# Weight transfers issued behind the first units' scaling, unit 0 first on every engine, and a second layer two units behind the first

## The chip, the cores and the metric

The kernel runs on one core of one Trainium2 chip. The metric is the device time in microseconds of that core; before the change three runs took 210.71, 210.63 and 213.97 us (median 210.71). The engines named below are PE (matmuls), ACT (activations), DVE (vector work), POOL (elementwise work, and the issue of the weight transfers) and SP (the issue of all other transfers). Each engine takes its instructions strictly in the order in which they are written.

## The reference, cut to what matters

A gated linear attention (a decayed state per head) feeds a two-layer perceptron with a leaky ReLU:

```python
# q, k, v, f_logit: (4, 8, 768, 48)
f = 1.0 / (1.0 + np.exp(-f_logit))
for t in range(S):
    state = f[:, :, t, :, None] * state + einsum('bhd,bhe->bhde', k[:, :, t], v[:, :, t])
    y[:, :, t] = einsum('bhd,bhde->bhe', q[:, :, t], state)
x = y.transpose(0, 2, 1, 3).reshape(B * S, H * D)       # 3072 x 384
h = x @ w_in                                            # 384 x 2048
g = np.maximum(0.01 * h, h)
return g @ w_out                                        # 2048 x 384
```

All inputs arrive as f32. The four attention inputs are 18.9 MB together, each weight matrix is 3.1 MB, and the output is 4.7 MB.

## The kernel before, in words

**Units.** The sequence of 768 steps is cut into 6 chunks of 128; a unit is one chunk of one of the 4 batch rows with all 8 heads, so there are 24 units, chunk by chunk. Units 0 to 3 are the first chunk of the four rows and have no state to read. A unit's four inputs f, k, q, v are four transfers of 192 KB each (`load`, L82), issued by SP, in runs of 48 f32 per head and step. Its output is one transfer of 192 KB (`put`, L261).

**Attention of a unit.** `gate_act` turns f into log decays lf with two activations; `gate_pe` sums them along the chunk with one matmul (into cs) and four narrow ones; `decay_act` makes the factors em and a (and a_end, but for the last chunk); `scale_pool` multiplies k by em (kh), q by a (qh) and casts v, all three on POOL. `turn_pe` transposes kh and qh on PE, `turn_dve` copies them out as kT and qbd; `score_pe` makes the scores pw, `mask_dve` masks them into wm, `mix_pe` makes the output py (for later chunks with the state too), `y_act` casts it to xn, `x_pe` transposes it, and `x_dve` copies it into xT, the input of the first layer. `state_pe`, `state_dve` and `state_pool` bring the state up to the end of the chunk.

**The two layers.** `up(u, g)` is one quarter of the first layer: 24 matmuls of 128x128 into one of two PSUM buffers pm, and one Prelu activation on ACT into gT. `down(u, half)` is half of the second layer: 8 matmuls of 128x384 into pm2, of which there is one buffer; `put` copies pm2 out on DVE and has SP store it. Of gT there are 5 buffers.

**Weights.** `load_w_in(part, 2)` issues three transfers of 256 KB on POOL (half of the columns, as bf16), `load_w_out(part, 2)` one of 768 KB. Groups 0 and 1 of `up` need the first half of w_in, groups 2 and 3 the second; the first half of `down` needs the first half of w_out.

**Order.** The order is written by hand (manual schedule): each engine's program is the order of the calls. Ahead of the loop stand the loads, then the attention of unit 0 mixed with the gates of units 1 and 2. The loop over units (L300 to L331) puts the attention of unit i+1 between the pieces of the two layers of unit i, the scaling of unit i+2 and the gate activations of unit i+3 beside them. `LA` is 5: `load(i + 5)` stands at the head of iteration i.

Of the kernel before, what the change touches and what calls it, by code (L numbers as in the profile page):

```python
# [15 lines left out]
def kernel(  # L16
# [10 lines left out]
    nc = tc.nc  # L27

    B, H, S, D = q.shape
# [9 lines left out]
    NU = len(units)  # L39
# [29 lines left out]
    qhs = [const.tile([128, H, 64], BF16, name=f"qh{i}", tag=f"qh{i}") for i in range(3)]  # L69
# [10 lines left out]
    raw = {}  # L80

    def load(u):  # L82
        c, b = units[u]
        r = {}
        for name, src in (("f", f_logit), ("k", k), ("q", q), ("v", v)):
            t = inp.tile([128, H, D], FP32, name=f"{name}_raw", tag=f"{name}_raw")
            nc.sync.dma_start(out=t, in_=src[b, :, c * C:(c + 1) * C, :].rearrange("h t d -> t h d"))
            r[name] = t
        raw[u] = r

    def load_w_in(part, parts):
        w = FF // parts
        for kk in range(NK):
            nc.gpsimd.dma_start(out=w_in_b[:, kk, part * w:(part + 1) * w],  # L94
                                in_=moe_w_in[kk * 128:(kk + 1) * 128, part * w:(part + 1) * w])

    def load_w_out(part, parts):
        n = NF // parts
        nc.gpsimd.dma_start(  # L99
            out=w_out_b[:, part * n:(part + 1) * n, :],  # L100
            in_=moe_w_out[part * n * 128:(part + 1) * n * 128, :].rearrange("(a p) n -> p a n", p=128))

    st = {}


    def gate_act(u):
        f = raw[u]["f"]
        e = work.tile([128, H, D], FP32, name="e_t", tag="e_t")
        nc.scalar.activation(e, f, AF.Exp, scale=-1.0)  # L109
        lf = lfs[u % 3]  # L110
        nc.scalar.activation(lf[:, :, 0:D], e, AF.Ln, bias=1.0)  # L111

    def gate_pe(u):
        c, b = units[u]
        lf = lfs[u % 3]
        cs = ps_s.tile([128, 512], FP32, name="cs", tag="sm")
        nc.tensor.matmul(cs[:, 0:H * D], ut, lf[:, :, 0:D], start=True, stop=True)  # L117
        if c < NCH - 1:
            for p in range(P2):
                nc.tensor.matmul(cs[:, H * D + p:H * D + p + 1], lf[:, 2 * p:2 * p + 2, :], ones_col,  # L120
                                 start=True, stop=True)
        st[u] = {"cs": cs}

    def decay_act(u):
        c, b = units[u]
        cs = st[u]["cs"]
        a_t = work.tile([128, H, D], BF16, name="a_t", tag="a_t")
        em_t = work.tile([128, H, D], BF16, name="em_t", tag="em_t")
        nc.scalar.activation(em_t, cs[:, 0:H * D], AF.Exp, scale=1.0)  # L129
        nc.scalar.activation(a_t, cs[:, 0:H * D], AF.Exp, scale=-1.0)  # L130
        if c < NCH - 1:
            a_end = work.tile([128, P2], FP32, name="a_end", tag="a_end")
            nc.scalar.activation(a_end, cs[:, H * D:H * D + P2], AF.Exp, scale=-1.0)
            st[u]["a_end"] = a_end
        st[u]["a"], st[u]["em"] = a_t, em_t

    def scale_pool(u):
        r = raw.pop(u)
        nc.gpsimd.tensor_mul(khs[u % 3][:, :, 0:D], r["k"], st[u]["em"])  # L139
        nc.gpsimd.tensor_mul(qhs[u % 3][:, :, 0:D], r["q"], st[u]["a"])  # L140
        v_b = work.tile([128, H, D], BF16, name="v_b", tag="v_b")
        nc.gpsimd.tensor_copy(out=v_b, in_=r["v"])  # L142
        st[u]["v"] = v_b

    def turn_pe(u):
        tp = ps_t.tile([128, 2, P2, 128], BF16, name="tp", tag="tp")
        for i, src in enumerate((khs[u % 3], qhs[u % 3])):
            for p in range(P2):
                nc.tensor.transpose(tp[:, i, p, :], src[:, 2 * p:2 * p + 2, :], ident)  # L149
        st[u]["tp"] = tp  # L150
# [27 lines left out]
    def mix_pe(u):  # L178
        c, b = units[u]
        s = st[u]  # L180
        qbd, v_b, wms = qbds[u % 2], s["v"], s.pop("wm")
        py = ps_s.tile([128, 512], FP32, name="py", tag="sm")
        n = H if c == 0 else 2 * H
        i = 0
        if c > 0:
            for h in range(H):
                nc.tensor.matmul(py[:, h * D:(h + 1) * D], qbd[:, h // 2, h % 2, :], state_b[b][:, h // 2, :],  # L187
                                 start=(i == 0), stop=(i == n - 1))
                i += 1
        for h in range(H):  # L190
            nc.tensor.matmul(py[:, h * D:(h + 1) * D], wms[h // 4][:, h % 4, :], v_b[:, h, :],  # L191
                             start=(i == 0), stop=(i == n - 1))
            i += 1
        s["py"] = py

    def state_pe(u):
        c, b = units[u]
        if c == NCH - 1:
            return
        kh, v_b = khs[u % 3], st[u]["v"]  # L200
        pt = ps_s.tile([128, P2, 2 * D], FP32, name="pt", tag="sm")
        for p in range(P2):
            nc.tensor.matmul(pt[:, p, :], kh[:, 2 * p:2 * p + 2, :], v_b[:, 2 * p:2 * p + 2, :],  # L203
                             start=True, stop=True)
        st[u]["pt"] = pt
# [18 lines left out]
    def y_act(u):  # L224
        xn = work.tile([128, KD], BF16, name="xn", tag="xn")
        nc.scalar.copy(out=xn, in_=st[u].pop("py")[:, 0:KD])  # L226
        st[u]["xn"] = xn

    def x_pe(u):
        xn = st[u].pop("xn")  # L230
        px = ps_s.tile([128, NK, 128], BF16, name="px", tag="sm")
        for kk in range(NK):
            nc.tensor.transpose(px[:, kk, :], xn[:, kk * 128:(kk + 1) * 128], ident)  # L233
        st[u]["px"] = px

    def x_dve(u):
        xT = work.tile([128, NK, 128], BF16, name="xT", tag="xT", bufs=6)
        nc.vector.tensor_copy(out=xT, in_=st[u].pop("px"))  # L238
        st[u]["xT"] = xT


    def up(u, g):
        s = st[u]
        if g == 0:
            s["g"] = gpool.tile([128, NF, 128], BF16, name="gT", tag="gT")
        pm = ps_m.tile([128, 4, 128], FP32, name="pm", tag="pm")
        for i in range(4):
            ff = 4 * g + i
            for kk in range(NK):
                nc.tensor.matmul(pm[:, i, :], w_in_b[:, kk, ff * 128:(ff + 1) * 128], s["xT"][:, kk, :],  # L250
                                 start=(kk == 0), stop=(kk == NK - 1))
        nc.scalar.activation(s["g"][:, 4 * g:4 * g + 4, :], pm, AF.Prelu, alpha=0.01)  # L252

    def down(u, half):
        s = st[u]
        if half == 0:
            s["pm2"] = ps_o.tile([128, KD], FP32, name="pm2", tag="pm2")
        for ff in range(8 * half, 8 * half + 8):
            nc.tensor.matmul(s["pm2"], s["g"][:, ff, :], w_out_b[:, ff, :], start=(ff == 0), stop=(ff == NF - 1))  # L259

    def put(u):  # L261
        c, b = units[u]
        osb = opool.tile([128, KD], FP32, name="osb", tag="osb")
        nc.vector.tensor_copy(out=osb, in_=st[u]["pm2"])  # L264
        nc.sync.dma_start(out=out[b * S + c * C:b * S + (c + 1) * C, :], in_=osb)
        st.pop(u)


    LA = 5
    load(0)  # L270
    load_w_in(0, 2)
    load(1)
    load_w_in(1, 2)
    load_w_out(0, 2)
    load_w_out(1, 2)
    for u in range(2, LA):
        load(u)

    gate_act(0)
    gate_act(1)  # L280
    gate_pe(0)
    decay_act(0)
    scale_pool(0)
    gate_pe(1)
    decay_act(1)
    scale_pool(1)
    gate_act(2)
    turn_pe(0)
    turn_dve(0)
    score_pe(0)  # L290
    mask_dve(0)
    mix_pe(0)
    state_pe(0)
    y_act(0)
    state_dve(0)
    state_pool(0)
    x_pe(0)
    x_dve(0)

    for i in range(NU):  # L300
        n1, n2, n3 = i + 1, i + 2, i + 3
        if i + LA < NU:
            load(i + LA)
        if n1 < NU:
            turn_pe(n1)
            turn_dve(n1)
        up(i, 0)
        up(i, 1)
        if n1 < NU:
            score_pe(n1)  # L310
            mask_dve(n1)
        if n2 < NU:
            gate_pe(n2)
            decay_act(n2)
            scale_pool(n2)
        up(i, 2)
        up(i, 3)
        if n1 < NU:
            mix_pe(n1)
            y_act(n1)  # L320
            state_pe(n1)
            state_dve(n1)
            state_pool(n1)
        if n3 < NU:
            gate_act(n3)
        down(i, 0)
        if n1 < NU:
            x_pe(n1)
            x_dve(n1)
        down(i, 1)  # L330
        put(i)  # L331


# [28 lines left out]
```

## Time and profile before

| | |
|---|---|
| three runs, us | 210.71, 210.63, 213.97 |
| the profiled execution, first to last instruction | span 209.4 us (its own device time is not listed; the two lowest runs are 1.2 and 1.3 us above this span) |
| busy: PE, ACT, DVE, POOL | 177.8, 108.7, 97.4, 76.8 us |
| first `up` matmul, last `down` matmul ends | 33.73 us, 206.08 us |
| DMA | 27.12 MB, of them 3.15 MB weights as written |
| granted clock of PE | 1.000 |

The profiler records one execution. Starts are microseconds from the first instruction of the span. In the view in order of time, a bracket at a row's end gives the idle time of that engine just before it, and what ended it. The chain of waits is followed back from the last instruction. The rows are shown in the prediction, where they are used.

### The profile page before, as it was taken

Reading aid. Unit: us, or ns where it says so; the run is one execution under the profiler, and the core shown is the slowest. Engines: PE = TensorE matmul, PEld = TensorE weight load, DVE = VectorE, ACT = ScalarE, POOL = GpSimd, SP = SyncE. Lnnn points to the kernel's source line nnn. Section 1 sums busy time; section 2 is a strip of 40 time slices with the busy share of each in tenths; the row PEclk is TensorE's granted clock in tenths of the full one; section 3 lists DMA queues with packets and bytes.
Section 4 is the critical chain, followed back from the end, with each engine's and each line's share of the span. In section 5 each row is a group of like instructions: output and inputs, shape, how many; then the busy total and the mean of one; then the engine's idle time right before and its main releaser. Section 6 shows DMA issues by size and latency. Waiting matters only on the chain.

```text
span 209.4 us, 5831 instructions
## 1 busy us (share of the span) xinstructions
PE 177.8 (85%) x2432; PEld 146.1 (70%) x2432; DVE 97.4 (46%) x223; ACT 108.7 (52%) x237; POOL 76.8 (37%) x129
## 2 busy tenths in 40 slices
PE   0000149999999999999999999999999999999993
PEld 0000028788779788877988887798888778877881
DVE  8000044466546545654654565465455545633511
ACT  4000332775576458447645845774585567555540
POOL 8300071542553255145325524532552454034000
PEclk9999999999999999999999999999999999999999
DMA  6999999998796479568647846956695681100111
GB/s 114 171 195 184 199 191 189 156 219 163 121 176 143 105 136 177 114 118 163 147 102 133 186 111 116 157 116 141 128 187 113 119 153 41 38 28 18 38 41 38
DMA packets 106267, 27.12 MB, mean 130 GB/s; under 512 B 100352, under 2 KB 105472, under 8 KB 106240
## 3 DMA queue, kind: packets, MB, share of 16 engines
q1 hardware_dynamic: 103296, 23.60, 59.5%
q0 software_dynamic: 2944, 3.15, 9.0%
q8 instruction: 19, 0.31, 0.6%
q14 instruction: 8, 0.07, 0.1%
HBM read 25.17 MB, written 4.72 MB: 143 GB/s over the span
## 4 chain that ended last, share of the span: by engine, by line
PE 83%; issue 10%; POOL 4%; DVE 1%; ACT 0%; POOLq 0%
PE pm L250 32%; PE pm L259 30%; PE pw L168 6%; PE tp L149 5%; PE py L191 2%; PE px L233 2%; PE py L187 2%; PE cs L117 2%; PE pt L203 2%; POOL w_in_b L94 2%; POOL w_out_b L99 1%; POOL kh L139 1%; PE cs L120 1%; DVE wm L175 1%; POOL qh L140 1%
## 5 line engine op out<-in xcount | busy, mean ns | idle before, releaser
L252 ACT ACTIVATE gT<-pm 128x512 bf16<-128x512 f32 x96 | 56.2, 601 | 64.1 <-PE pm L250 62.3
L250 PE MATMUL pm<-xT,w_in_b 128*128 128x128 bf16 x1152 | 73.4, 221 | 0.0
L259 PE MATMUL pm<-w_out_b,gT 128*128 128x384 bf16 x384 | 70.1, 326 | 0.0
L250 PEld LDWEIGHTS <-w_in_b 128*128 128x128 bf16 x1152 | 67.2, 99 | 0.6
L139 POOL TENSOR_TENSOR kh<-k_raw,em_t 128x384 bf16<-128x384 f32 x24 | 22.0, 916 | 110.5 <-ACT em_t L129 105.7
L259 PEld LDWEIGHTS <-gT 128*128 128x128 bf16 x384 | 35.2, 98 | 18.8
L175 DVE TENSOR_TENSOR wm<-pw,ut 128x512 bf16<-128x512 f32 x48 | 30.9, 686 | 12.7 <-PE pw L168 11.9
L117 PE MATMUL cs<-lf,ut 128*128 128x384 bf16 x24 | 8.1, 339 | 24.9 <-ACT lf L111 24.9
L264 DVE COPY osb<-pm 128x384 f32<-128x384 f32 x24 | 13.4, 558 | 26.6 <-PE pm L259 26.6
L109 ACT ACTIVATE e_t<-f_raw 128x384 f32<-128x384 f32 x24 | 12.9, 536 | 23.7 <-DMA f_raw<-in_f_logit_dram 23.7
L120 PEld LDWEIGHTS <-lf 128*128 128x128 bf16 x80 | 5.0, 99 | 25.2 <-issue 23.8
L140 POOL TENSOR_TENSOR qh<-q_raw,a_t 128x384 bf16<-128x384 f32 x24 | 21.9, 914 | 0.0
L155 DVE COPY kT<-tp 128x512 bf16<-128x512 bf16 x24 | 10.0, 415 | 23.6 <-PE tp L149 23.6
L238 DVE COPY xT<-px 128x384 bf16<-128x384 bf16 x24 | 8.6, 358 | 22.2 <-PE px L233 22.2
L213 DVE TENSOR_TENSOR sf<-sf,pt 64x192 f32<-64x192 f32 x20 | 6.9, 346 | 22.2 <-PE pt L203 22.2
L168 PE MATMUL pw<-qbd,kT 128*128 128x256 bf16 x96 | 14.8, 277 | 1.3 <-DVE qbd L158 1.3
L129 ACT ACTIVATE em_t<-cs 128x384 bf16<-128x384 f32 x24 | 11.8, 491 | 4.5 <-PE cs L120 3.7
L111 ACT ACTIVATE lf<-e_t 128x384 bf16<-128x384 f32 x24 | 12.5, 523 | 0.8
L168 PEld LDWEIGHTS <-kT 128*128 128x128 bf16 x96 | 9.4, 99 | 4.3 <-DVE kT L155 0.8
L226 ACT CAST xn<-py 128x384 bf16<-128x384 f32 x24 | 11.4, 474 | 1.5 <-PE py L191 1.5
L142 POOL CAST v_b<-v_raw 128x384 bf16<-128x384 f32 x24 | 12.1, 505 | 0.0
L130 ACT ACTIVATE a_t<-cs 128x384 bf16<-128x384 f32 x24 | 11.6, 485 | 0.0
(37 smaller groups left out, 155.3 us busy)
## 6 DMA issues: line engine op xcount, KB each, us to landing
f_raw<-in_f_logit_dram SPq DMA_DIRECT2D x24, 192.0 KB, 3.2
k_raw<-in_k_dram SPq DMA_DIRECT2D x24, 192.0 KB, 3.8
q_raw<-in_q_dram SPq DMA_DIRECT2D x24, 192.0 KB, 4.0
v_raw<-in_v_dram SPq DMA_DIRECT2D x24, 192.0 KB, 4.3
out_dram<-osb SPq DMA_DIRECT2D x24, 192.0 KB, 2.0
w_in_b<-in_moe_w_in_dram POOLq DMA_DIRECT2D x6, 256.0 KB, 8.8
w_out_b<-in_moe_w_out_dram POOLq DMA_DIRECT2D x2, 768.0 KB, 18.2
```

The source lines that it names most:

```text
L109: nc.scalar.activation(e, f, AF.Exp, scale=-1.0)
L111: nc.scalar.activation(lf[:, :, 0:D], e, AF.Ln, bias=1.0)
L117: nc.tensor.matmul(cs[:, 0:H * D], ut, lf[:, :, 0:D], start=True, stop=True)
L139: nc.gpsimd.tensor_mul(khs[u % 3][:, :, 0:D], r["k"], st[u]["em"])
L140: nc.gpsimd.tensor_mul(qhs[u % 3][:, :, 0:D], r["q"], st[u]["a"])
L142: nc.gpsimd.tensor_copy(out=v_b, in_=r["v"])
L168: nc.tensor.matmul(pw[:, 2 * i:2 * i + 2, :], kT[:, p, :], qbd[:, p, :, :], start=True, stop=True)
L175: nc.vector.tensor_mul(wm, pw, ut[:, None, :].to_broadcast([128, 4, 128]))
L250: nc.tensor.matmul(pm[:, i, :], w_in_b[:, kk, ff * 128:(ff + 1) * 128], s["xT"][:, kk, :], start=(kk == 0), stop=(kk == NK - 1))
L252: nc.scalar.activation(s["g"][:, 4 * g:4 * g + 4, :], pm, AF.Prelu, alpha=0.01)
L259: nc.tensor.matmul(s["pm2"], s["g"][:, ff, :], w_out_b[:, ff, :], start=(ff == 0), stop=(ff == NF - 1))
L264: nc.vector.tensor_copy(out=osb, in_=st[u]["pm2"])
```

## The change

Four things are moved; the arithmetic stays as it was.

1. All five opening loads are issued by SP one after the other, and the weight transfers are issued by POOL later: the first half of w_in behind unit 0's qh, the second half behind its v cast, the first half of w_out behind unit 1's v cast, the second half behind unit 2's.
2. `scale_pool` is split into `scale` and `cast_v`; for units 0 and 1 the multiplication of k goes from POOL to DVE.
3. Ahead of the loop, unit 0's attention is written whole before anything of unit 1, then `up(0, ...)` is mixed with the attention of unit 1. The loop begins at i = 1.
4. `down` and `put` belong to unit i-2 (`LAG = 2`), and the loop runs two iterations longer. The load at the head of iteration i is that of unit i+4.

```diff
-    def scale_pool(u):
+    def scale(u):
+        r = raw[u]
+        eng = nc.vector if u < 2 else nc.gpsimd
+        eng.tensor_mul(khs[u % 3][:, :, 0:D], r["k"], st[u]["em"])
+        nc.gpsimd.tensor_mul(qhs[u % 3][:, :, 0:D], r["q"], st[u]["a"])
+
+    def cast_v(u):
         r = raw.pop(u)
-        nc.gpsimd.tensor_mul(khs[u % 3][:, :, 0:D], r["k"], st[u]["em"])
-        nc.gpsimd.tensor_mul(qhs[u % 3][:, :, 0:D], r["q"], st[u]["a"])
         v_b = work.tile([128, H, D], BF16, name="v_b", tag="v_b")
         nc.gpsimd.tensor_copy(out=v_b, in_=r["v"])
...
     LA = 5
-    load(0)
-    load_w_in(0, 2)
-    load(1)
-    load_w_in(1, 2)
-    load_w_out(0, 2)
-    load_w_out(1, 2)
-    for u in range(2, LA):
+    LAG = 2
+    for u in range(LA):
         load(u)
     gate_act(0)
-    gate_act(1)
     gate_pe(0)
     decay_act(0)
-    scale_pool(0)
-    gate_pe(1)
-    decay_act(1)
-    scale_pool(1)
-    gate_act(2)
+    scale(0)
+    load_w_in(0, 2)
+    cast_v(0)
+    load_w_in(1, 2)
     turn_pe(0)
     turn_dve(0)
     score_pe(0)
     mask_dve(0)
     mix_pe(0)
+    y_act(0)
+    x_pe(0)
+    x_dve(0)
     state_pe(0)
...
+    gate_act(1)
+    gate_pe(1)
+    decay_act(1)
+    up(0, 0)
+    up(0, 1)
+    scale(1)
+    cast_v(1)
+    load_w_out(0, 2)
+    up(0, 2)
+    up(0, 3)
+    turn_pe(1)
+    turn_dve(1)
+    gate_act(2)
+    gate_pe(2)
+    score_pe(1)
+    mask_dve(1)
+    decay_act(2)
+    scale(2)
+    cast_v(2)
+    load_w_out(1, 2)
+    mix_pe(1)
+    y_act(1)
+    x_pe(1)
+    x_dve(1)
+    state_pe(1)
+    state_dve(1)
+    state_pool(1)
+    gate_act(3)
+
-    for i in range(NU):
+    for i in range(1, NU + LAG):
...
-        if i + LA < NU:
-            load(i + LA)
+        if i + LA - 1 < NU:
+            load(i + LA - 1)
...
-        down(i, 0)
+        if d >= 0:
+            down(d, 0)
...
-        down(i, 1)
-        put(i)
+        if d >= 0:
+            down(d, 1)
+            put(d)
```

On POOL, at the head of its work (the numbers at kh and qh are buffers, w_in_b and w_out_b the weights, sf and sb the state), there stood before:

```order
L62 MEMSET ones_col 128x1
L94 DMA w_in_b<-in_moe_w_in_dram 128x1024 x6
L99 DMA w_out_b<-in_moe_w_out_dram 128x8x384 x2
L139 TENSOR_TENSOR kh_108<-k_raw,em_t 128x8x48
L140 TENSOR_TENSOR qh_105<-q_raw,a_t 128x8x48
L142 CAST v_b<-v_raw 128x384
L139 TENSOR_TENSOR kh_109<-k_raw,em_t 128x8x48
```

And now, at the same place:

```order
L62 MEMSET ones_col 128x1
L141 TENSOR_TENSOR qh_105<-q_raw,a_t 128x8x48
L94 DMA w_in_b<-in_moe_w_in_dram 128x1024 x3
L146 CAST v_b<-v_raw 128x384
L94 DMA w_in_b<-in_moe_w_in_dram 128x1024 x3
L225 TENSOR_TENSOR sf_113<-sf_113,a_end 128x192
L226 CAST sb_117<-sf_113 128x192
L141 TENSOR_TENSOR qh_106<-q_raw,a_t 128x8x48
L146 CAST v_b<-v_raw 128x384
L99 DMA w_out_b<-in_moe_w_out_dram 128x8x384
```

The weights were the first thing that POOL issued; now each part stands behind work that waits for a load, and the kh of units 0 and 1 is gone from POOL.

On ACT, behind the load of its table (e_t and lf are the gate of a unit, em_t, a_t and a_end its decay, xn its attention output), there stood before:

```order
L109 ACTIVATE e_t<-f_raw 128x384
L111 ACTIVATE lf_102<-e_t 128x8x48
L109 ACTIVATE e_t<-f_raw 128x384
L111 ACTIVATE lf_103<-e_t 128x8x48
L129 ACTIVATE em_t<-cs 128x384
L130 ACTIVATE a_t<-cs 128x384
L133 ACTIVATE a_end<-cs 128x4
```

And now:

```order
L109 ACTIVATE e_t<-f_raw 128x384
L111 ACTIVATE lf_102<-e_t 128x8x48
L129 ACTIVATE em_t<-cs 128x384
L130 ACTIVATE a_t<-cs 128x384
L133 ACTIVATE a_end<-cs 128x4
L230 CAST xn<-py 128x384
L109 ACTIVATE e_t<-f_raw 128x384
L111 ACTIVATE lf_103<-e_t 128x8x48
```

Unit 1's gate, which waits for unit 1's f, stood ahead of unit 0's decay, and now stands behind unit 0's attention.

On DVE, at the end of its program (osb is the copy of a unit's pm2, xT the last unit's first-layer input), there stood before:

```order
L175 TENSOR_TENSOR wm<-pw,ut 128x512 x2
L238 COPY xT<-px 128x384
L264 COPY osb<-pm_3813 128x384
L264 COPY osb<-pm_3896 128x384
L357 UNCONDITIONAL_BRANCH
```

And now:

```order
L179 TENSOR_TENSOR wm<-pw,ut 128x512 x2
L242 COPY xT<-px 128x384
L268 COPY osb<-pm_3773 128x384
L268 COPY osb<-pm_3856 128x384
L268 COPY osb<-pm_3876 128x384
L268 COPY osb<-pm_3896 128x384
L388 UNCONDITIONAL_BRANCH
```

The copies of the last units stand one behind the other: behind the last `up` there are three second layers where there was one.

More of the change, by code (lines that the diff above doesn't have):

```diff
@@ L292 @@
     mix_pe(0)
+    y_act(0)
+    x_pe(0)
+    x_dve(0)
     state_pe(0)
-    y_act(0)
     state_dve(0)
     state_pool(0)
-    x_pe(0)
-    x_dve(0)
-    for i in range(NU):
-        n1, n2, n3 = i + 1, i + 2, i + 3
-        if i + LA < NU:
-            load(i + LA)
+    gate_act(1)
[27 more added lines that the diff above has]
+    for i in range(1, NU + LAG):
+        n1, n2, n3, d = i + 1, i + 2, i + 3, i - LAG
+        if i + LA - 1 < NU:
+            load(i + LA - 1)
         if n1 < NU:
@@ L306 @@
             turn_dve(n1)
-        up(i, 0)
-        up(i, 1)
+        if i < NU:
+            up(i, 0)
+            up(i, 1)
         if n1 < NU:
@@ L314 @@
             decay_act(n2)
-            scale_pool(n2)
-        up(i, 2)
-        up(i, 3)
+            scale(n2)
+            cast_v(n2)
+        if i < NU:
+            up(i, 2)
+            up(i, 3)
         if n1 < NU:
```

## The prediction

> **What bounds the kernel now.** I read the page's slices first, then the chain of waits, then the opening in order of time, then the DMA queues by stretch.
>
> ```profile
> span 209.4 us, 5831 instructions
> PE   0000149999999999999999999999999999999993
> DMA  6999999998796479568647846956695681100111
> ```
>
> PE is idle for the first 26 us or so and full afterwards; the DMA engines are full for the first 42 us or so. The chain says the same in steps (start, length):
>
> ```profile
> 7.00 18.85 issue
> ...
> 33.94 2.56 PE pm L250 x24
> ...
> 42.14 1.34 PE pm L250 x24
> ...
> 44.29 1.36 PE pm L250 x24
> 46.02 1.30 PE pm L259 x8
> 47.49 1.30 PE pm L259 x8
> ...
> 49.24 1.34 PE pm L250 x24
> ...
> 206.08 0.56 DVE osb L264
> ```
>
> From 33.94 to 206.08 it is PE and nothing else: 172.14 us of work. An iteration of the first chunk is 42.14 to 49.24, 7.10 us, of which the two halves of `down` are 2.60. Only the opening can give time. What fills it:
>
> ```profile
> 1.23 0.57 SPq L87 DMA_DIRECT2D k_raw<-in_k_dram  x1
> ...
> 3.73 0.52 ACT L109 ACTIVATE e_t<-f_raw 128x384 f32<-128x384 f32 x1 [1.71 <-DMA f_raw<-in_f_logit_dram]
> 3.83 4.72 SPq L87 DMA_DIRECT2D f_raw<-in_f_logit_dram  x1
> ...
> 5.13 0.29 PE L120 MATMUL cs<-ones_col,lf 128*128 128x1 bf16 x4
> ...
> 24.35 0.52 ACT L109 ACTIVATE e_t<-f_raw 128x384 f32<-128x384 f32 x1 [19.54 <-DMA f_raw<-in_f_logit_dram]
> ...
> 25.33 0.47 ACT L129 ACTIVATE em_t<-cs 128x384 bf16<-128x384 f32 x1
> ...
> 25.70 0.48 ACT L130 ACTIVATE a_t<-cs 128x384 bf16<-128x384 f32 x1
> ...
> 26.76 0.91 POOL L140 TENSOR_TENSOR qh<-q_raw,a_t 128x384 bf16<-128x384 f32 x1
> ...
> 27.72 0.61 PE L149 MATMUL tp<-ident,qh 128*128 128x128 bf16 x4 [0.26 <-POOL qh L140]
> ...
> 33.73 2.77 PE L250 MATMUL pm<-xT,w_in_b 128*128 128x128 bf16 x24
> ...
> 37.05 1.50 PE L250 MATMUL pm<-xT,w_in_b 128*128 128x128 bf16 x24
> ```
>
> Unit 0's sums are ready at 5.42, but its decay stands on ACT behind unit 1's gate, and that gate's f, issued at 3.83, lands at 24.35: 20.5 us for 192 KB. The transfer waited because the weights were moving. First the six w_in transfers, then the two of w_out (issue and landing), then the queues from 4 to 16 us, 16 to 26 us and 27 to 37 us (packets, MB, share):
>
> ```profile
> L94 POOL DMA_DIRECT2D w_in_b<-in_moe_w_in_dram x6: 548/562/744, 1.8 to 4.6; - x6
> DMA to landing us min/median/max: 4.5/8.8/11.1
> L99 POOL DMA_DIRECT2D w_out_b<-in_moe_w_out_dram x2: 947/950/952, 5.2 to 6.0; - x2
> DMA to landing us min/median/max: 15.9/18.2/20.5
> ...
> q0 software_dynamic: 1157, 1.78, 84.3%
> q1 hardware_dynamic: 2027, 0.39, 23.8%
> ...
> q0 software_dynamic: 1769, 1.33, 84.9%
> q1 hardware_dynamic: 3016, 0.57, 42.3%
> ...
> q1 hardware_dynamic: 10117, 1.91, 127.2%
> ```
>
> The pipe carries 2.17 MB in 12 us, 1.90 in 10, 1.91 in 10: 181 to 191 GB/s whatever is in it (186 below). While w_in is in it, weights take 148 GB/s and loads 32; beside w_out it is 133 and 57; a load of 0.197 MB alone takes 1.0 us.
>
> **The change part by part.** The sum needs one date: when `up` of unit 2 can start with PE full from there on.
>
> Step 1, unit 0 first. Its decay follows 5.42 at once: em at 5.5, a 0.37 later, 0.48 long, so 6.35. Its k, issued at 1.23, landed 3.7 us later:
>
> ```profile
> DMA to landing us min/median/max: 3.7/3.7/3.7
> ```
>
> That is 4.9, and q one load later, 5.9, with no weights in the way. The qh of 0.91 us then ends at 7.3 instead of 27.67. The kh on DVE is not in the trace. The nearest rows, a DVE copy and a DVE product, bound it:
>
> ```profile
> L238 DVE COPY xT<-px 128x384 bf16<-128x384 bf16 x24 | 8.6, 358 | 22.2 <-PE px L233 22.2
> L175 DVE TENSOR_TENSOR wm<-pw,ut 128x512 bf16<-128x512 f32 x48 | 30.9, 686 | 12.7 <-PE pw L168 11.9
> ```
>
> At 0.36 to 0.69 us beside the qh of 0.91 it costs nothing; without that cover it would cost its own 0.7.
>
> Step 2, w_in late. Its first issue goes from 1.8 to 7.3. Before, its last part landed at 4.6 + 11.1 = 15.7, 13.9 after the first issue; the same lag gives 21.2. By rate: 1.57 MB at 148 GB/s is 10.6 us; with about 2 us ahead of the first bytes (f of unit 0 took 3.0, of which 1.0 is transfer) 19.9. I take 20.5. Unit 0's xT comes 33.73 - 27.72 = 6.0 us after qh, at 13.3; `up(0)` waits for w_in, not for unit 0.
>
> Step 3, to `up(1)`. Groups 2 and 3 of `up(0)` start at 20.5 and take the slow 2.77: 23.3. Then unit 1's transposes: 0.4 for kh and the 6.0 from qh to `up`, so 29.7. The gate of unit 2 lies within that, in DVE's part. The loads it needs, at the shares above: until 9.3, when weights flow, 6.6 loads are in; q of unit 1 at about 12, v at 18; the first half of w_out is issued at 18.6 and flows from 20 to 26 (0.79 MB at 133 GB/s); f of unit 2 at 22, q at 27, v at 28. What is queued behind these waits on POOL is just the next part of the weights. They are in time.
>
> Step 4, to `up(2)`. In a full iteration qh of the unit after next ends 45.83 + 0.91 - 42.14 = 4.60 us after `up` starts:
>
> ```profile
> 45.83 0.91 POOL L140 TENSOR_TENSOR qh<-q_raw,a_t 128x384 bf16<-128x384 f32 x1
> ...
> 48.83 0.56 DVE L264 COPY osb<-pm 128x384 f32<-128x384 f32 x1 [0.94 <-PE pm L259]
> ```
>
> With 0.3 for the last transposes 4.9; slow matmuls add up to 1.2 (2.77 against 1.50); I take 5.5, so 35.2. But there is a second bound. The last half of w_out is issued behind unit 2's v, about 28.5, and f of unit 4 has 17 loads and all weights ahead of it or with it: 3.34 + 3.15 MB at 186 GB/s from 2.7 is 37.6. Its gate takes 0.5 + 0.5 and stands on ACT ahead of the first Prelu of `up(2)` (0.6), whose PSUM buffer group 2 needs: 39.3. Group 2 comes 44.29 - 42.14 = 2.15 after group 0. So PE is full as from a start at 37.1. The later bound decides: 37.0, from 34.5 (the pipe helps the loads first) to 39.5 (matmuls slow throughout, the pipe 2 us short).
>
> Step 5, what is left. Of 172.14 us, the two iterations 33.94 to 49.24 (15.30) are done, save their two `down`, 5.20: 162.04. The steady iteration keeps the same instructions on every engine, and the chain shows no wait of PE in it, so lagging `down` frees nothing there.
>
> By the Trainium skill, TensorE: Matmul & The Clock Gate, "What's actually happening", PE falls back to half rate after an idle window of about 3.4 us and needs as long a busy one to leave it. The trace agrees with the two rates (2.77 against 1.50 for the same 24 matmuls) though the granted clock reads 1.00 throughout; by that rule a long wait just ahead of `up(2)` would put back 1.3 us, so 206.2 in all.
>
> Step 6, the tail. Behind the last `up` stand three second layers with one pm2 buffer, and two of them wait for the copy before: from the last matmul at 47.49 + 1.30 = 48.79 to the copy at 48.83, 0.56 of copy, and some 0.05 back, 0.65 each: 1.3 that was covered by `up` before. SP's stores get no longer.
>
> Sum: 37.0 + 162.0 + 1.3 = 200.3 against 206.08, that is -5.8. The tail behind is the same copy and store: span 203.6 for 209.4. The two lower runs lie 1.2 and 1.3 above the span, so 210.71 - 5.8 = 204.9.
>
> **The rivals.** A, equal shares: loads and weights split the pipe evenly. Then w_in at 93 GB/s takes 16.9 us, lands at 26.2, `up(1)` starts at 35.4, `up(2)` at 40.9, and the end comes at 204.2: 208.8 us. Against it: with both queues backed up weights had 1.78 of 2.17 MB. The Trainium skill, DMA: Bandwidth & Descriptors, "Queues, rings and completion order", says that each DMA engine takes turns between queues packet by packet, which gives equal shares only for equal packets; the trace's shares are far from equal. Chance 0.13.
>
> B, the opening is worse by 2 to 3 us: the pipe idles between the four weight parts, or PE runs slow into `up(2)`. A start at 39.1 gives 207.0. For it: each part now waits for a load and for POOL. Against: five loads are queued all along. Chance 0.17.
>
> C, slower: loads starve and the weights wait for them. The v of unit 0 shows what a load behind weights can take:
>
> ```profile
> DMA to landing us min/median/max: 16.3/16.3/16.3
> ```
>
> If v of unit 1 takes 16.3 us more than alone, it lands at 25, the first half of w_out is issued at 25.5, v of unit 2 then suffers the same and lands near 43, and the last half of w_out, at its landing of 15.9, near 59.5. The first `down` stands 5 us behind the start of `up(2)` and would hold PE from 42 to 59.5: about 222. It makes the kernel slower by 2% once that half lands after 52. Against: one part of w_out is a quarter of what then lay ahead. Chance 0.05.
>
> D, that the weights do not move, is excluded: POOL's new program has them behind qh and the casts.
>
> **How the numbers follow.** My forecast (203 to 206.5) has 0.60, the better opening (below 203) 0.05, A 0.13, B 0.17, C 0.05. Two per cent, what a measurement here tells from no change, is 206.5 and 214.9. Faster: 0.65. Within: A and B, 0.30. Slower: C, 0.05. The range runs from 202.4 (start at 34.5) to 208.8 (A); left out are C, and the farther halves of A and of the better opening, about 0.15.
>
> **What would show it.** The first `up` near 15.5 and group 2 near 20.5; `up(2)` at 35 to 37; from there no PE wait but two of 0.65 us at the end; the last matmul near 200.3; f of unit 1 landing before 9 rather than at 24.35. I am wrong if the first w_in half lands after 19, if loads beside the weights take well over 6 us each, or if `down` of unit 0 waits for w_out.

## The result, and the profile after

The changed kernel took 205.17 us (median of four runs, 203.58 to 206.17), the kernel before 211.77 beside it (210.63 to 213.97): a ratio of 0.972, 95% interval 0.966 to 0.977. The forecast was 204.9, or 5.8 below before; measured beside it the difference is 6.6. The profiled execution took 205.08 us, span 203.3 against 209.4.

The page's slices of the changed kernel:

```profile
span 203.3 us, 5831 instructions
PE   0446778999999999999999999999999999999973
DMA  6999999999976946865874785595585671110111
```

PE has work from about 6 us on, where it had none until 26. The DMA row reads 9 from its second to its eleventh slice, to 56 us, where it did so to its ninth, 47 us (not 42, as the prediction read it): the opening is still filled by transfers. The chain of waits of the changed kernel (start, length):

```profile
7.26 1.75 POOL w_in_b L94 x3
10.49 10.41 DMA w_in_b<-in_moe_w_in_dram
20.95 2.54 PE pm L254 x22
30.18 2.23 PE pm L254 x24
36.30 1.50 PE pm L254 x24
38.48 1.36 PE pm L254 x24
...
190.52 2.61 PE pm L263 x16
...
197.18 2.77 PE pm L263 x16
```

The end is now followed back to w_in. Before, the chain led into 18.85 us called "issue" on POOL, in which unit 0's scaling stood behind the late f of unit 1. The last part of w_in is issued at 10.49 and lands at 20.9; `up(1)` starts at 30.0 to 30.2, `up(2)` at 36.30, and the last matmul ends at 199.95. Before, that end was 206.08.

The changed kernel in order of time, at the places that the forecast dated:

```profile
6.36 0.91 POOL L141 TENSOR_TENSOR qh<-q_raw,a_t 128x384 bf16<-128x384 f32 x1 [4.50 <-ACT a_end L133]
16.30 0.96 POOL L99 DMA_DIRECT2D w_out_b<-in_moe_w_out_dram  x1
16.67 2.63 PE L254 MATMUL pm<-xT,w_in_b 128*128 128x128 bf16 x23 [1.22 <-DMA w_in_b<-in_moe_w_in_dram]
36.35 0.52 ACT L109 ACTIVATE e_t<-f_raw 128x384 f32<-128x384 f32 x1 [0.90 <-DMA f_raw<-in_f_logit_dram]
193.16 0.56 DVE L268 COPY osb<-pm 128x384 f32<-128x384 f32 x1 [4.90 <-PE pm L263]
193.77 2.76 PE L263 MATMUL pm<-w_out_b,gT 128*128 128x384 bf16 x16 [0.65 <-DVE osb L268]
```

The qh of unit 0 ends at 7.27 (27.67 before). The fourth row is the second bound of the forecast: ACT waited 0.90 us for unit 4's f, which landed at 36.3. The last two rows are a wait of the tail.

### The profile page after: what moved, and what is told of

Read it like the earlier page. It is cut to its first block, busy times and chain, and to the rows that moved or that the text cites. A ratio compares the mean times of both kernels' runs of the same rounds, so it can differ in the third digit from the quotient of the medians.

```text
span 203.3 us, 5831 instructions
## 1 busy us (share of the span) xinstructions
PE 183.2 (90%) x2432; PEld 149.2 (73%) x2432; DVE 98.6 (48%) x225; ACT 109.2 (54%) x237; POOL 75.3 (37%) x127
## 4 chain that ended last, share of the span: by engine, by line
PE 85%; DMA 7%; ACT 3%; POOL 2%; DVE 1%; issue 1%
PE pm L254 32%; PE pm L263 31%; PE pw L172 6%; DMA w_in_b<-in_moe_w_in_dram 5%; PE tp L153 5%; PE py L195 2%; PE px L237 2%; PE cs L117 2%; PE py L191 2%; PE pt L207 2%; DMA f_raw<-in_f_logit_dram 1%; POOL w_in_b L94 1%; DVE osb L268 1%; PE cs L120 1%; DVE wm L179 1%
## 5 line engine op out<-in xcount | busy, mean ns | idle before, releaser
L254 PE MATMUL pm<-xT,w_in_b 128*128 128x128 bf16 x1152 | 76.0, 224 | 3.9 <-DMA w_in_b<-in_moe_w_in_dram 3.9
L254 PEld LDWEIGHTS <-w_in_b 128*128 128x128 bf16 x1152 | 69.2, 101 | 5.4 <-DMA w_in_b<-in_moe_w_in_dram 4.7
L140 POOL TENSOR_TENSOR kh<-k_raw,em_t 128x384 bf16<-128x384 f32 x22 | 20.1, 915 | 93.0 <-ACT em_t L129 88.2
L263 PEld LDWEIGHTS <-gT 128*128 128x128 bf16 x384 | 35.4, 98 | 20.9 <-issue 1.8
L217 DVE TENSOR_TENSOR sf<-sf,pt 64x192 f32<-64x192 f32 x20 | 6.9, 346 | 20.9 <-PE pt L207 19.3
L225 POOL TENSOR_TENSOR sf<-sf,a_end 128x192 f32<-128x192 f32 x20 | 10.1, 505 | 3.7 <-DVE sf L218 3.7
```

Source lines behind the costliest of these rows:

```text
L140: eng.tensor_mul(khs[u % 3][:, :, 0:D], r["k"], st[u]["em"])
```

## The experiments

All ratios are to the kernel before, run beside each on the same chip; e1 to e4 shared one chip, e5 to e10 another. The changed kernel itself did not run beside e1 to e4. Theories about dates are read from the profiles, since the times of one kernel scatter by 1 to 2%.

**e1: the order alone.** The kernel before, its weights at POOL's head, without lag; unit 0's attention is written whole ahead of unit 1's gate.

```diff
     gate_act(0)
-    gate_act(1)
     gate_pe(0)
     decay_act(0)
     scale_pool(0)
-    gate_pe(1)
-    decay_act(1)
-    scale_pool(1)
-    gate_act(2)
     turn_pe(0)
...
     x_dve(0)
+    gate_act(1)
+    gate_pe(1)
+    decay_act(1)
+    scale_pool(1)
+    gate_act(2)
```

> The kernel before, with the weights still first on POOL and no lag, but unit 0's attention written whole ahead of unit 1's gate on every engine. My theory (the order alone frees unit 0 from unit 1's f, and the loop then waits for unit 1's q, which landed at 27.7 us in the kernel before): qh of unit 1 ends near 28.7, the first matmul of up(0) comes at 29.2 instead of 33.7, PE is full from there, and the end is 4.6 us earlier: about 206 us against 210.7. Rival (the gain needs the late weights): up(0) starts within 1 us of where it was and the time stays within 1 us of before.

It took 208.85 us against 213.12: 0.981 (0.973 to 0.988), that is -4.3 us. In order of time:

```profile
26.25 0.52 ACT L109 ACTIVATE e_t<-f_raw 128x384 f32<-128x384 f32 x1 [3.70 <-DMA f_raw<-in_f_logit_dram]
30.79 2.77 PE L250 MATMUL pm<-xT,w_in_b 128*128 128x128 bf16 x24
```

Unit 1's f landed 1.9 us later in this run than in the first profile of before (24.35), and `up(0)` started 1.6 later than the 29.2 expected, 2.9 earlier than before (33.73). The last matmul ends at 204.1, 1.9 earlier than in the one profile of before, which is from another chip. The rival falls: the order alone gains, with the weights where they were. How much is less sure: the interval of the times is 2.5 to 5.7 us, and that they give nearly the 4.6 expected, though the dates gave less, is in part chance.

**e2: the new order, the weights at the head again.**

```diff
+    load_w_in(0, 2)
+    load_w_in(1, 2)
+    load_w_out(0, 2)
+    load_w_out(1, 2)
     for u in range(LA):
         load(u)
...
     scale(0)
-    load_w_in(0, 2)
     cast_v(0)
-    load_w_in(1, 2)
...
     cast_v(1)
-    load_w_out(0, 2)
...
     cast_v(2)
-    load_w_out(1, 2)
```

> The changed kernel, with all weight transfers back at the head of POOL's program, the rest (order, lag, kh on DVE) as changed. My theory (the new order starts up(0) only when unit 1's f is in, and leaves unit 1's attention behind up(0)): f of unit 1 lands near 24 as in the kernel before, up(0) starts at 26, up(1) at 37, up(2) at 42 instead of 36.3, the last matmul ends near 205.6 instead of 200.0: about 210 us, as slow as before. Rival (the pipe carries the same bytes in any order, so the issue order of the weights is worth nothing): up(2) starts at 36 to 37 and the time stays at 205.

212.77 us, 0.996 (0.990 to 1.001): no gain. PE's largest wait (us in total, times, longest):

```profile
PE tp L153 <- POOL qh L141: 10.3, 1, 10.3
```

And the start of `up(2)`, in order of time:

```profile
43.91 1.50 PE L254 MATMUL pm<-xT,w_in_b 128*128 128x128 bf16 x24
```

The 10.3 us are PE waiting between unit 0's kh and qh, since q of unit 0 sat behind the weights. `up(0)`, `up(1)`, `up(2)` started at 28.0, 38.0 and 43.9 (expected 26, 37, 42, with f of unit 1 at 26.4 instead of 24), and 43.91 + 163.6 is the end, 207.5. So the bytes are the same, but which come first decides; the rival falls.

**e3: no lag.**

```diff
-    LAG = 2
+    LAG = 0
...
     gate_act(3)
+    down(0, 0)
+    down(0, 1)
+    put(0)
```

> The changed kernel with no lag: down(0) stands ahead of the loop and down(i) in iteration i. My theory (the lag is what lets PE go on while the last half of w_out is on its way): that half lands at 38 to 39, PE stands still from about 30 until then, up(1) starts near 40, and the last matmul ends near 204 instead of 200.0: about 209 us. Rival (the lag only costs its two waits in the tail): the same opening, 1.3 us earlier at the end, about 203.8.

211.78 us, 0.993 (0.989 to 0.998). The two halves of `down(0)` in order of time:

```profile
29.36 2.52 PE L263 MATMUL pm<-w_out_b,gT 128*128 128x384 bf16 x8
39.20 2.71 PE L263 MATMUL pm<-w_out_b,gT 128*128 128x384 bf16 x8 [7.32 <-DMA w_out_b<-in_moe_w_out_dram]
```

Two windows of the same run (length; busy time and number of instructions of PE, its weight loads PEld, DVE, ACT and POOL; granted clock, DMA share, GB/s):

```profile
31.00:40.00 9.00, 1.68 (x7) 0.76 (x6) 0.00 (x0) 0.00 (x0) 0.37 (x2) 0.69 1.20 191
40.00:43.00 3.00, 3.00 (x19) 2.02 (x18) 0.75 (x2) 0.00 (x0) 0.00 (x0) 0.50 0.04 8
```

PE waited 7.3 us for the last half of w_out, which landed at 39.2 as expected. `up(1)` started at 42.6, not 40: the matmuls behind the wait ran at about half rate (2.71 for 8 that take 1.46, granted clock 0.50), which I had not counted, nor the 8 matmuls and the transposes ahead of `up(1)` themselves. The first half was slow too (2.52), ahead of the wait. With the weights late, the gain needs the lag; the rival, that the lag only costs, falls.

**e4: the tail without its waits.** Unit 22's pm2 is taken from the scores' PSUM buffers.

```diff
+            if u == NU - 2:
+                s["pm2"] = ps_w.tile([128, KD], FP32, name="pm2", tag="pw")
+            else:
                 s["pm2"] = ps_o.tile([128, KD], FP32, name="pm2", tag="pm2")
```

> The changed kernel with the second layer of unit 22 in a PSUM buffer of the scores instead of pm2, so that neither of the last two second layers waits for a copy. My theory: the two waits of 0.64 us go, the last matmul ends 1.3 us earlier behind the start of up(2), about 203.9 us. Rival (the copy is hidden by the pipelining of the matmuls, the waits in the trace are not on the path): no change.

204.7 us, 0.962 (0.954 to 0.969). Its chain:

```profile
39.33 0.53 ACT e_t L109
39.91 0.40 issue
40.32 0.59 ACT gT L256
40.95 1.50 PE pm L254 x24
...
193.10 7.81 PE pm L266 x48
```

The 48 matmuls of the last three `down` run without a gap in 7.81 us; in the changed kernel they span 190.52 to 199.95, 9.43. From the third group of `up(2)` to the last matmul it is 200.91 - 40.95 = 159.96, against 199.95 - 38.34 = 161.61 (38.34 is that group's first matmul in order of time; the chain has 38.48): 1.65 less, of which 1.3 was expected. The tail accounts for 9.43 - 7.81 = 1.62: two waits of 0.65, and 16 matmuls behind each that take 2.77 instead of 2.61. The opening, though its program is the same, was later: unit 4's f landed at 39.3 instead of 36.3, and the chain runs through its gate and the Prelu behind it to PE, as step 4 had it.

**e5: the changed kernel again.** No edit.

> The changed kernel again, unaltered, on the chip on which the next ones run. In the run with the altered tail f of unit 4 landed at 39.3 us, 3 us later than in the first profile of the changed kernel, and the second half of up(2) waited behind it. My theory (the opening is bound by the pipe through that f): wherever this f lands, the third group of up(2) starts 1.7 to 2.2 us behind it or, where it is early, 2.2 behind the start of up(2), and the last matmul ends 161.5 us after that group's start (163.65 - 2.15). Rival (PE's own chain is the bound): the date of f makes no difference to the start of that group, which stays at 38.5.

205.89 us, 0.975 (0.968 to 0.983). The first and the third group of `up(2)`:

```profile
37.23 1.50 PE L254 MATMUL pm<-xT,w_in_b 128*128 128x128 bf16 x24
39.27 1.50 PE L254 MATMUL pm<-xT,w_in_b 128*128 128x128 bf16 x24
```

Here the f landed at 29.7 + 6.6 = 36.3, early, and the third group came 2.04 us behind the first; from it to the last matmul's end (200.86) it is 161.6. Where f was late (39.3 in e4, 38.5 in e10) the group came 1.6 us behind it, just under the 1.7 to 2.2 expected, and not at 38.5: the rival falls. Both bounds are real, and which decides differs from run to run.

**e6: a lag of one.**

```diff
-    LAG = 2
+    LAG = 1
```

> The changed kernel with a lag of one unit. My theory: the first second layer now stands ahead of up(2), and its second half waits for the last half of w_out, landing at 38 to 39: up(2) starts near 40.5, with one second layer (2.6) already done and one tail wait (0.64) less, so that the last matmul ends between 1.5 us earlier and 1 us later than with a lag of two, the earlier where f of unit 4 is late. Rival (each unit of lag is worth half of what the whole lag was worth, some 7 us between no lag and two): 3 us slower.

206.17 us, 0.979 (0.968 to 0.990): 0.3 us above e5, inside what the runs scatter. Its profile, the longest of its runs, in order of time:

```profile
38.41 2.72 PE L263 MATMUL pm<-w_out_b,gT 128*128 128x384 bf16 x8 [3.24 <-DMA w_out_b<-in_moe_w_out_dram]
41.77 2.66 PE L254 MATMUL pm<-xT,w_in_b 128*128 128x128 bf16 x24
```

A window of it, with the columns of e3:

```profile
35.00:45.00 10.00, 6.76 (x53) 5.15 (x51) 2.40 (x6) 1.43 (x3) 0.61 (x2) 0.66 1.09 197
```

The wait for w_out is 3.2 us, as the landing at 38 says, and again the matmuls behind it are slow: `up(2)` starts at 41.77, 1.3 later than expected, and in this execution the last matmul ends at 203.2, 2.3 behind e5. By the times one unit of lag does nearly all that two do, as my theory had it; in the one profiled execution the loss was near the rival's 3 us. That is not settled beyond the scatter.

**e7: unit 4's gate out of the way**, with e4's tail. In iteration 2 unit 4's gate activations, until then at the end of iteration 1, come behind the Prelu activations of `up(2)`, and its sums and scaling behind the first half of `down(0)`.

```diff
-        if n2 < NU:
+        if n2 < NU and i != 2:
             gate_pe(n2)
...
             up(i, 3)
+        if i == 2:
+            gate_act(n2)
...
-        if n3 < NU:
+        if n3 < NU and i != 1 and i != 2:
             gate_act(n3)
...
             down(d, 0)
+        if i == 2:
+            gate_pe(n2)
+            decay_act(n2)
+            scale(n2)
+            cast_v(n2)
+            gate_act(n3)
```

> The altered tail, and in iteration 2 alone unit 4's gate behind the Preludes of up(2) on ACT, with its sums and scaling behind the first half of down(0), so that neither waits for unit 4's f ahead of PE's own work. My theory (the f of unit 4 reaches PE through ACT's order): the third group of up(2) starts 2.2 us behind the first whenever f lands; where f lands at 39, the end is 1 to 2 us earlier than that of the run with the altered tail alone, where it lands at 36, it is the same or 0.5 us later (unit 4's turn waits for its scaling). Rival (the same f holds PE a little later just as long, at the sums of unit 4): no gain in either case.

205.17 us, 0.971 (0.963 to 0.980). In order of time:

```profile
38.88 1.50 PE L254 MATMUL pm<-xT,w_in_b 128*128 128x128 bf16 x24
...
43.91 0.91 POOL L141 TENSOR_TENSOR qh<-q_raw,a_t 128x384 bf16<-128x384 f32 x1
44.88 0.40 PE L153 MATMUL tp<-ident,qh 128*128 128x128 bf16 x4 [0.47 <-POOL qh L141]
```

The third group came 1.8 us behind the first (37.11), free of ACT's order. But unit 4's scaling, moved behind, then held its transposes: `up(3)` started 8.0 us behind `up(2)`, where e5 has 7.0. The rival has it: the wait moved on, and no gain over e4 shows in the times (0.971 and 0.962).

**e8: kh of units 0 and 1 on POOL.** It ran once.

```diff
-        eng = nc.vector if u < 2 else nc.gpsimd
+        eng = nc.gpsimd
```

> The changed kernel with kh of units 0 and 1 back on POOL, ahead of qh. My theory: qh of unit 0 ends 0.5 to 0.9 us later, the first issue of w_in moves from 7.2 to about 7.7 to 8.1, and w_in's last part lands and the third group of up(0) starts that much later; the end moves by no more than that, and by nothing where unit 4's f is the bound. Rival (kh on DVE is what frees unit 0): up(0) starts over 2 us later.

```profile
7.19 0.91 POOL L141 TENSOR_TENSOR qh<-q_raw,a_t 128x384 bf16<-128x384 f32 x1
...
22.18 2.53 PE L254 MATMUL pm<-xT,w_in_b 128*128 128x128 bf16 x22 [1.21 <-DMA w_in_b<-in_moe_w_in_dram]
```

Against e5, qh starts 0.61 us later (7.19 for 6.58), the second half of `up(0)` 0.65 later (22.18 for 21.53), the last matmul ends 0.89 later (201.75 for 200.86); the single time is 206.87. DVE's kh took 0.56 us in the changed kernel's profile, inside the bounds 0.36 to 0.69. In the seven profiles with this opening and kh on DVE (the first of the changed kernel, e3 to e7 and e10), qh started at 6.36 to 6.64 and the second half of `up(0)` at 20.95 to 21.56, so both delays lie outside the scatter of the dates: w_in's issue stands behind qh. The rival, over 2 us, falls. What it costs at the end, some 0.6 to 0.9 us, one execution does not settle.

**e9: PE's waits in the opening filled**, with e4's tail. The work is the same, its order is:

```diff
     up(0, 0)
     up(0, 1)
     scale(1)
     cast_v(1)
     load_w_out(0, 2)
-    up(0, 2)
-    up(0, 3)
     turn_pe(1)
     turn_dve(1)
+    up(0, 2)
+    score_pe(1)
+    mask_dve(1)
+    up(0, 3)
...
+        if i < NU:
+            up(i, 0)
+            up(i, 1)
+            if i == 1:
+                up(i, 2)
+                up(i, 3)
         if n1 < NU:
             turn_pe(n1)
             turn_dve(n1)
-        if i < NU:
-            up(i, 0)
-            up(i, 1)
+        if n2 < NU and i != 2:
+            gate_act(n2)
+        if i < NU and i != 1:
+            up(i, 2)
+            up(i, 3)
+        if i == 2:
+            gate_act(n2)
+        if n2 < NU and i > 2:
+            gates(n2)
...
```

Here `gates(u)` is `gate_pe`, `decay_act`, `scale` and `cast_v` of a unit.

> The altered tail, and PE's order filled where it waited in the opening: unit 1's transposes, scores and mask stand between the quarters of up(0), the whole of up(1) ahead of unit 2's transposes, in the loop the transposes of the next unit behind the first two quarters of up, the gate of the unit after next behind them on ACT, its sums behind the last quarter, and a unit's x transposes in the middle of the second half of down. The work is the same. My theory (between the landing of w_in near 21 and the start of up(2) near 36.5 PE's own chain is the longest, with 4 us of waits in it, and the f of unit 4 holds only ACT's order): up(2) starts near 33.5, up(3) 2 to 3 us earlier than the 44.2 of the unaltered kernel, the last matmul ends between 196 and 198.5, the time is 201 to 203.5. Rival (the pipe is the bound: unit 4's q lands at 40 to 43 whatever PE does): up(3) starts no earlier than 43.5 and only the 1.3 us of the tail are gained, about 204.5.

206.38 us, 0.969 (0.963 to 0.975), no better than e10 beside it (0.958). In order of time:

```profile
32.97 0.60 PE L172 MATMUL pw<-qbd,kT 128*128 128x256 bf16 x4 [1.30 <-DVE qbd L162]
...
34.14 0.27 PE L195 MATMUL py<-v_b,wm 128*128 128x48 bf16 x4 [0.33 <-DVE wm L179]
...
36.38 2.33 PE L254 MATMUL pm<-xT,w_in_b 128*128 128x128 bf16 x24 [0.46 <-DVE xT L242]
```

`up(1)` started at 26.9, 3 us earlier, and `up(2)` no earlier at 36.4. My theory falls: with `up(1)` done before unit 2's transposes, the chain of one unit, from its transposes at 31.06 to its xT, has nothing to cover it, and PE waits in each of its steps (the brackets); the first group of `up(2)` behind these waits is slow too, 2.33 for 1.50. `up(3)` started at 45.5, later than in e5; so the rival's bound, 43.5, is kept, but unit 4's loads are not shown to be its cause.

**e10: the altered tail again**, beside e9. No edit against e4.

> The run with the altered tail again, to stand beside the filled order on the same chip. Theory: 1.3 us less than the unaltered changed kernel behind the same opening, 203.5 to 204.7 us, and no wait for a copy at the end.

204.24 us, 0.958 (0.951 to 0.964). Unit 4's f was late again:

```profile
38.52 0.52 ACT L109 ACTIVATE e_t<-f_raw 128x384 f32<-128x384 f32 x1 [2.17 <-DMA f_raw<-in_f_logit_dram]
...
40.13 1.50 PE L254 MATMUL pm<-xT,w_in_b 128*128 128x128 bf16 x24
```

Twice, this version has the lowest median: 204.7 and 204.24 against 205.17 and 205.89 for the changed kernel. The difference, 0.5 to 1.65 us, lies inside the scatter of the times; that the two waits of 0.65 are gone is shown by the traces.

## Why the prediction was right, point by point

**The bound before** was the order and the late f of unit 1 together. e1 shows that the order alone gains (4.3 us by the medians, 1.9 by the profiles) with the f as late as ever. The prediction put the gain down to both and did not see that the order would pay without the late weights.

**Step 1** (qh of unit 0 at 7.3): 7.27. That kh on DVE "costs nothing" held; e8 adds that leaving it on POOL would have cost 0.6 or more at w_in's landing.

**Step 2** (w_in's second half at 20.5): 20.95. The first matmul of `up(0)` came at 13.6 and the bulk of them at 16.67, where 15.5 was forecast for the first.

**Step 3** (`up(1)` at 29.7): 30.0. Its account of the loads was wrong inside: v of unit 1 landed at 11.0, not 18, since SP had sent all eight loads of units 0 and 1 before the weights flowed. The first half of w_out was issued at 16.3 rather than 18.6, held by POOL's order, not by a load. That q and v of unit 2 landed at 27.2 and 28.3, as forecast (27, 28), is partly luck: the two errors ran against each other.

**Step 4** (`up(2)` at 37.0, as the later of 35.2 and 37.1): 36.30. The forecast had the f of unit 4 decide; in this profile PE's own chain did. It took 6.1 by the chain's dates (30.18 to 36.30), the slow end of the 4.9 to 6.1 given, where 5.5 was taken, and not by the link that was dated. Unit 3's qh ended at 35.48, which with the 0.3 of its transposes makes 35.8; PE waited for unit 2's xn, and `up(2)` for the xT made from it:

```profile
35.51 0.34 PE L237 MATMUL px<-ident,xn 128*128 128x128 bf16 x3 [0.69 <-ACT xn L230]
```

In the iterations behind it a half of `down` stands ahead of these transposes and no such wait shows; in iteration 1 the lag leaves none there. The f of unit 4 landed at 36.3 instead of 37.6, which makes the second bound 35.8 instead of 37.1. So the first bound came 1.1 late and the second 1.3 early, and that the sum missed by only 0.7 is partly luck. In e4 and e10 this f landed at 39.3 and 38.5 and then was the bound, which is rival B's start of 39.1 (40.95 - 2.04 = 38.9 in e4).

**Steps 5 and 6** (162.0 and 1.3): from 36.30 to 199.95 it is 163.65 against 163.3, and the two waits of the tail are 0.65 each. No other wait of PE appears behind the opening in the view of waits. The sum was 200.3; the end came at 199.95, an error of -0.7 in the start and +0.35 behind it.

**What was left open**: that the lag "frees nothing" in the steady iterations held, but its worth in the opening was only implied. e3 puts it at 7.3 us of waiting for w_out.

**The rivals.** A, equal shares, is refuted by the queues of the changed kernel from 10 to 20 us:

```profile
q0 software_dynamic: 844, 1.53, 87.4%
q1 hardware_dynamic: 1402, 0.27, 19.7%
```

Weights had 1.53 of 1.80 MB. C, weights held back by starved loads, did not occur: v of unit 2 held POOL for 0.16 us ahead of the last half of w_out, no half of w_out took more than 10.3 us to land, and the last was in at 39.1 at the latest, before its `down` at 41.5. The loads beside the weights were slow all the same: f, k, q and v of unit 2, issued between 7.5 and 17.7, took 13.5, 16.0, 17.0 and 10.6 us to land. By that count the sign "well over 6 us each" did show, and it did not mean what the prediction took it for; one behind the other they landed 1.1 to 3.5 us apart (21.0, 24.5, 27.2, 28.3), in time for PE. B was seen in part, as said.

**PE's slow rate.** Behind 7.3 us of waiting in e3 and 3.2 in e6, 8 matmuls of `down` took 2.71 and 2.72 us instead of 1.46; the granted clock was 0.50 from 40 to 43 us in e3 and 0.66 on average from 35 to 45 in e6. The slow rate also came without such a wait: in e3 PE was slow ahead of it, in the first half of `down(0)` (2.52), with no wait over 0.9 us in the 5 us before. The Trainium skill, TensorE: Matmul & The Clock Gate, "What's actually happening", says that PE falls to half rate after an idle window of about 3.4 us. e3's long wait agrees with it; e6's is a little shorter, and the slow half ahead of e3's wait is not covered by it. What set that off is open. Ahead of `up(2)` the changed kernel had no wait over 0.7 us, `up(2)` ran at full rate, and the sum, which left out the 1.3 us, held.

## What to carry to other kernels

When an opening waits for a transfer, look first at what stands ahead of the waiting instruction in its engine's order: here the first unit was held by the second unit's gate, and a new order alone gained (ratio 0.981). Of the whole change, though, little is left when one part is taken out: 0.996 with the weights first, where PE waits 10.3 us for unit 0's q, and 0.993 without the lag, where it waits 7.3 us for w_out. Late weights with the old order were not run. So date each landing and each engine's place, take the later bound, and count it again for every part that is left out. A wait moved out of one place (e7, e9) turned up in the next chain each time.

## What the runs showed that was not expected

The pipe (the DMA engines together) is not the same from run to run: from 20 to 30 us the same opening moved 195 GB/s in the first profile of the changed kernel and 177 and 178 in e5 and e4. Unit 4's f landed at 36.3 in the first two and at 39.3 in e4, where the pipe moved 175 GB/s from 30 to 40 us too and the others 193. Nor was it always full: in the changed kernel, with loads and weights both issued, it fell for 4 us, which no run explains (windows, with the columns of e3):

```profile
8.00:10.00 2.00, 0.78 (x4) 0.50 (x4) 1.22 (x4) 0.00 (x0) 2.00 (x5) 1.00 1.41 189
10.00:12.00 2.00, 0.92 (x10) 0.42 (x8) 1.20 (x2) 0.36 (x1) 1.04 (x2) 1.00 0.97 142
12.00:14.00 2.00, 1.52 (x13) 0.97 (x13) 1.02 (x3) 1.31 (x4) 0.10 (x1) 1.00 0.99 148
14.00:16.00 2.00, 0.29 (x1) 0.10 (x1) 0.56 (x1) 0.69 (x3) 1.94 (x4) 1.00 1.13 202
```

And a wait of PE can cost more than its length: behind the 3.2 us in e6, the next 8 matmuls of `down` and the first 24 of `up` took 2.72 and 2.66 us, where 1.46 and 1.50 are usual, 2.4 us more.
